# Loading K and V of a decode step in 32 transfers of 4 MB instead of 64 of 2 MB, with the second MLP matrix in four pieces instead of five

## The chip, the cores and the metric

The kernel runs on one core of a Trainium2 chip. The metric is the time of one execution on the device in microseconds (us); several executions are taken and the median is given. A core has a matrix engine (TensorE, here PE), a vector engine (DVE), a scalar engine (ACT), a general engine (POOL) and a queue engine (SP) that issues most of the transfers. Sixteen DMA engines carry every transfer between the chip's memory (HBM) and the core's on-chip memory (SBUF, 128 partitions); matmul results go to PSUM. A transfer is cut into packets that the sixteen engines work off, each in its own order, and its completion is counted engine by engine: the data may be used when the last of the sixteen is through.

## The reference

One decode step for eight sequences mixes sliding-window attention over a cache (branch A) with a small MLP (branch B), by a gate:

```
W = 2048; keys and values are the last W positions of caches of 8192
q = (x @ wq)                        # x: 8 x 576, wq: 576 x 4096 = 32 query heads of 128
scores = q . k / sqrt(128)          # 16 key/value heads, each serves 2 query heads
a = softmax(scores) @ v, then @ wo  # wo: 4096 x 576
b = gelu(layernorm(x) @ w1 + b1) @ w2 + b2     # w1: 576 x 4608, w2: 4608 x 576
out = g * a + (1 - g) * b,  g = sigmoid(sum(x * gate_w))
```

All inputs and the output are bf16. For each of 16 heads K is 8 batches x 2048 positions x 128 values, 4 MB (1 MB = 1,048,576 bytes here), and V the same: 128 MB together. wq is 4.5 MB, w1 and w2 5.06 MB each, wo 4.5 MB.

## The kernel before, in words

**Memory.** One large SBUF buffer, RAW, is cut into nine slots of SE = 8192 bf16 elements per partition (16 KB per partition, 2 MB over 128 partitions; L194, L195, L264, `slot` L338). At the start its lower part holds wq (slots 0 to 2) and w1 (from slot 3 on, L341 to L344); when the matmuls that read these are done (`o_qp` for wq, `o_hp` for w1), the slots take cache data. Slots 6 to 8 are free from the beginning.

**The stream.** A list (L557 to L565) fixes the order of all transfers on SP: six K units, then two V units, two K units and so on; after every eight V units comes a chunk of wo (W, 1.125 MB), and at the end the bias b2 and w2 (M) in pieces of 12, 12, 6, 4 and 2 rows per partition (`M_CUTS`, L564). A unit is one head and four of its eight batches: partition p holds the 64 consecutive positions x = p // 4 of batch p % 4, one contiguous run of 16,384 bytes (`src_of`, L580). Item n of the stream uses slot (n + 6) % 9 (`take_slot`, L584), so nine items share the nine slots in turn. SP issues the transfers in list order. Before each it waits until the former user of the slot is done (`slot_free`): for K that is the second of the unit's two transposes, for V the PV matmuls of the head, for wo and w2 their matmuls.

**K** (`k_unit`, L622): when a unit has landed, DVE transposes it in two steps (L641, 128 x 2048 fp32 words each) into one of two buffers KT, and PE multiplies each half with the queries (L650, L658 and, through a helper that keeps the loaded weights, L175). Four small POOL copies per unit (L634) lay out the queries for it; their source q4 is written by four ACT copies (L507). Scores of two heads (a group g: four units) share four PSUM banks.

**Softmax** (`softmax`, L589): after the fourth unit of a group, DVE takes the maximum (L592) and combines it (L595 to L601), ACT takes the exponential (L606), DVE transposes the result (L611), PE sums (L615). The next group's first score matmul waits for the exponentials, since the banks are shared.

**V** (`v_unit`, L670): after the second unit of a head PE multiplies the probabilities with both units (L684, 32 matmuls, `pv`). After the second head of a group, DVE and PE gather and scale the output (L697 to L707), and matmuls with wo (L550, `AccGroup`) add it to the result in PSUM. Matmuls with w2 (also L550) add to the same bank, a piece at a time as it lands. In the end the result is copied (L759, L760) and written out (L762).

**Order of work.** A planner (`_Plan.schedule`, L62) has an estimate of each operation's cost and of the transfers (428 GB/s) and lists every engine's operations by estimated earliest start, with a bonus for priority. The lists are fixed at build time; at run time each engine works through its own list in order and waits on semaphores where needed.

The selection matrices selv and seln (L459 to L464) and q4 carry the order in which batches lie on the partitions.

Of the kernel before, what the change touches and what calls it, by code (L numbers as in the profile page):

```python
# [181 lines left out]
def build_kernel(nc, A_x, A_k_cache, A_v_cache, A_wq, A_wo, B_x, B_w1, B_b1, B_w2, B_b2, gate_w, out):  # L182
# [8 lines left out]
    SCALE = float(Dh) ** -0.5  # L191
    HG = 2
    NG = Hkv // HG
    NSLOT = 9  # L194
    SE = 4 * W  # L195
    FC, FT = 4, 36
    FCW = 32 * FT
    HN = 3
# [10 lines left out]
    with ExitStack() as es:  # L209
# [51 lines left out]
        req("PT", 2 * 2048, BF)  # L261
        req("P", 2048, BF)
        req("KT", 2 * SE // 2, BF)
        req("RAW", NSLOT * SE, BF, 512)  # L264
        over("x_sb", "PT", 0, D, BF)
        over("gw_sb", "PT", 1152, D, BF)
        over("y_bf", "PT", 2304, D, BF)
# [67 lines left out]
        b1c = view("b1c", FC)  # L335

        def slot(s):
            return RAW[:, s * SE:(s + 1) * SE]  # L338

        wq_m = RAW[:, 0:4 * 4096].rearrange("p (t c) -> p t c", t=4)  # L340
        wq_r = RAW[:, 4 * 4096:4 * 4096 + 2048]  # L341
        W1O = 3 * SE
        w1_m = RAW[:, W1O:W1O + 4 * F].rearrange("p (t c) -> p t c", t=4)
        w1_r = RAW[:, W1O + 4 * F:W1O + 4 * F + F // 2]  # L344

# [11 lines left out]
        OC = 64  # L357

        eng_sems = {e: es.enter_context(nc.semaphore("sem_" + e)) for e in ENGS}
        dma_keys = ["x", "b", "b2", "wq", "w1", "out", "outb"] + ["s%d" % i for i in range(NSLOT)] + ["t%d" % i for i in range(4)]  # L360
        dma_sems = {k: es.enter_context(nc.semaphore("dma_" + k)) for k in dma_keys}

        P = _Plan()
# [92 lines left out]
        o_selv, o_seln = [], []  # L456
        for l in range(2):
            for h in range(2):
                for nm, lst in (("iqm", o_selv), ("i32", o_seln)):  # L459
                    def fn(e, l=l, h=h, nm=nm):  # L460
                        dst = bass.AP(arena_f, offset=foffs("selv" if nm == "iqm" else "seln") + 64 * l + 32 * h, ap=[[AST // 2, 128], [8, 4], [1, 8]])
                        src = bass.AP(arena_f, offset=foffs(nm) + 16 * l + h, ap=[[AST // 2, 128], [0, 4], [2, 8]])
                        return e.tensor_copy(dst, src)
                    lst.append(add("pool", fn, deps=[o_iqm] + o_i32, name="%s%d%d" % ("selv" if nm == "iqm" else "seln", l, h), cost=0.2, prio=-1))  # L464


        def held_x(e, out_of, lhs, rhs_of, n, t, first, last):
# [34 lines left out]

        o_q4 = []
        for he in range(4):
            def fn(e, he=he):
                src = bass.AP(ps, offset=BK_SEL * 512 + 8 * he, ap=[[PST, 128], [64, 16], [1, 8], [32, 2]])
                return e.activation(out=q4[:, he, :].rearrange("p (l b h) -> p l b h", l=16, b=8), in_=src, func=ACTF.Copy)  # L507
            o_q4.append(add("act", fn, deps=[o_selp], name="q4_%d" % he, cost=0.4))


        def h_fn(e):
# [42 lines left out]
                acc_groups.append(self)  # L554


        NUQ = 4 * NG  # L557
        stream = [("K", i) for i in range(6)]
        for vi in range(0, NUQ, 2):
            stream += [("V", vi), ("V", vi + 1)]  # L560
            if (vi + 2) % (NUQ // (Hq // WO_CH)) == 0:
                stream.append(("W", vi // (NUQ // (Hq // WO_CH))))
            stream += [("K", i) for i in (vi + 6, vi + 7) if i < NUQ]
        M_CUTS = [[12], [12], [6, 4, 2]]  # L564
        stream += [("B", 0)] + [("M", i) for i in range(len(M_CUTS))]  # L565

        last_dma = [d_w1r]
        slot_free = [[o_qp]] * 3 + [[o_hp]] * 3 + [[]] * 3
        n_slot = [0]
        tr_hist, qk_half = [], []  # L570
        qk_unit = {}
        exp_done, pt_done, pv_last = {}, {}, {}
        rg_done = {}
        o_item_ev = {}
        v_load, acc_ev, u_sum = {}, {}, {}
        b6_w, b6_r = [], [o_u]
        proj_ops = {}
        oT_done = {}

        def src_of(cache, g, q):  # L580
            hkv, b0 = 2 * g + q // 2, 4 * (q % 2)
            return cache[b0:b0 + 4, hkv, S0:Sk, :].rearrange("a (x r) d -> x a (r d)", x=32)

        def take_slot():  # L584
            n = n_slot[0]
            n_slot[0] += 1
            return (n + 6) % NSLOT

        def softmax(g):  # L589
            k = lambda i, n=1, parts=128, p0=0: sm[p0:p0 + parts, g, i:i + n]  # L590
# [28 lines left out]
            rg_done[g] = add("dve", lambda e: e.tensor_tensor(out=rg[:, g % 2:g % 2 + 1], in0=rr, in1=gcol, op=ALU.mult),  # L619
                             deps=[rc, o_gcol] + ([o_item_ev[g - 2]] if g >= 2 else []), name="rg_%d" % g, cost=0.16, prio=5)  # L620

        def k_unit(i):  # L622
            g, q = divmod(i, 4)
            s = take_slot()
            d = dma("sp", lambda e: e.dma_start(slot(s), src_of(A_k_cache, g, q)), "s%d" % s, 4 * W * Dh * 2, deps=slot_free[s], name="dk%d" % i, after=last_dma[-1:])
            last_dma.append(d)
            ub = q
            qrs = []
            for q_ in (q, q + 1) if q % 2 == 0 else ():
                for a in range(4):  # L630
                    def fn(e, a=a, q_=q_):
                        dst = bass.AP(arena, offset=32 * a * AST + aoffs("qbd") + q_ * 512 + 32 * a + 8 * q_, ap=[[AST, 32], [128, 4], [1, 8]])
                        src = bass.AP(arena, offset=32 * a * AST + aoffs("q4") + 32 * g + 8 * q_, ap=[[AST, 32], [256, 4], [1, 8]])
                        return e.tensor_copy(dst, src)  # L634
                    qrs.append(add("pool", fn, deps=o_q4 + [o_qz, qk_unit.get(4 * g + q_ - 4)], name="qr%d_%d" % (4 * g + q_, a), cost=0.2))
            trs = []
            for h in range(2):
                n = 2 * i + h
                kb = n % 2
                deps = [d] + ([qk_half[n - 2]] if n >= 2 else [o_selp])  # L640
                tr = add("dve", (lambda h=h, kb=kb: lambda e: e.transpose(bass.AP(arena_f, offset=foffs("KT") + kb * 2048, ap=[[AST // 2, 128], [1, 2048]]),  # L641
                                                                         bass.AP(arena_f, offset=foffs("RAW") + s * (SE // 2) + 32 * h, ap=[[AST // 2, 128], [64, 64], [1, 32]])))(),
                         deps=deps, name="tr%d_%d" % (i, h), cost=2.3, after=tr_hist[-1:])
                tr_hist.append(tr)
                trs.append(tr)

                def qk_fn(e, h=h, kb=kb):
                    mm = None
                    if q == 0 and h == 0:
                        e.matmul(ps[:, 0, :], maskL, maskR, start=True, stop=False)  # L650
                        for rc in range(1, 4):
                            held_matmul(nc, e, ps[:, rc, :], maskL, maskR, start=True, stop=False)
                    for ee in range(2):
                        for rc in range(4):
                            rhs = bass.AP(arena, offset=aoffs("KT") + kb * 4096 + rc * 1024 + ee, ap=[[AST, 128], [2, 512]])
                            args = (ps[:, rc, :], qbd[:, ub, 2 * h + ee, :], rhs)
                            last = q == 3 and h == 1 and ee == 1
                            mm = e.matmul(*args, start=False, stop=last) if rc == 0 else held_matmul(nc, e, *args, stop=last)  # L658
                    return mm
                deps = [tr] + qrs  # L660
                if q == 0 and h == 0:
                    deps += exp_done[g - 1] if g else o_q4 + [o_qs, o_mL, o_mR]
                qk = add("pe", qk_fn, deps=deps, name="qk%d_%d" % (i, h), cost=1.95 + (0.9 if q == 0 and h == 0 else 0), after=qk_half[-1:])
                qk_half.append(qk)
            qk_unit[i] = qk
            slot_free[s] = trs
            if q == 3:
                softmax(g)

        def v_unit(i):  # L670
            g, q = divmod(i, 4)
            s = take_slot()
            d = dma("sp", lambda e: e.dma_start(slot(s), src_of(A_v_cache, g, q)), "s%d" % s, 4 * W * Dh * 2, deps=slot_free[s], name="dv%d" % i, after=last_dma[-1:])  # L673
            last_dma.append(d)
            v_load[i] = (s, d)
            if i % 2 == 0:
                return

            def pv_fn(e):
                mm = None  # L680
                for t in range(16):
                    for j in (i - 1, i):
                        c = 32 * (j % 4)
                        mm = e.matmul(ps[c:c + 32, BK_OS[g % 2], :], PT[:, g % 2, 16 * c + 32 * t:16 * c + 32 * t + 32], slot(v_load[j][0])[:, 512 * t:512 * t + 512],  # L684
                                      start=(t == 0), stop=(t == 15), skip_group_check=True, tile_position=(0, c))
                return mm
            deps = [v_load[i - 1][1], d] + pt_done[g] + ([acc_ev[g - 2]] if g >= 2 else [o_u])
            prev = add("pe", pv_fn, deps=deps, name="pv%d" % i, cost=3.6, after=pv_hist[-1:])
            pv_hist.append(prev)
            slot_free[s] = slot_free[v_load[i - 1][0]] = [prev]  # L690
            if q == 3:
                pv_last[g] = prev
                for r in range(4):
# [15 lines left out]
                                 deps=[o_item_ev[g]], name="oT%d" % g, cost=0.25, prio=9)  # L709

        def wo_chunk(i):
            s = take_slot()
            h0 = WO_CH * i
            NT = WO_CH // WOR
            dst = slot(s)[:, 0:WO_CH * D].rearrange("p (t j c) -> p t j c", t=NT, j=WOR)
# [17 lines left out]
        def m2_chunk(ci):  # L733
# [12 lines left out]
                j, at = j + jn, at + jn  # L746
            slot_free[s] = ops

        pv_hist = []
        for kind, i in stream:  # L750
            {"K": k_unit, "V": v_unit, "W": wo_chunk, "M": m2_chunk, "B": bias}[kind](i)

        acc_ops = [g_.op for g_ in acc_groups]
        fin = []
# [78 lines left out]
```

## Time and profile before

| | |
|---|---|
| median of 3 runs | 367.55 us (367.52 to 367.84) |
| profiled execution | 367.57 us, its span 365.5 us |
| mean granted clock of PE | 0.860 |
| busy: PE / DVE / POOL / ACT | 246.3 / 225.7 / 36.1 / 31.9 us |
| HBM read | 154.31 MB, 422 GB/s over the span |
| K loads | 32, 2048 KB each, median 35.0 us from issue to landing |
| V loads | 32, 2048 KB each, median 33.4 us from issue to landing |

Here the page counts a KB as 1024 bytes and a MB as a million. "Busy" is time in which an engine worked; since engines overlap, the shares don't add up. The page's two lines of 40 digits or numbers cut the span into equal slices of 9.14 us: the DMA digits are the busy share of the sixteen DMA engines in tenths, GB/s is what they moved. "Issue to landing" includes the time that a transfer stands behind others in the queue. The chain of work is followed back from the last instruction, at each step to what released it. "SPq" and "PEq" stand for an engine's sequencer, where transfers are issued and waits take place.

### The profile page before, as it was taken

To read this page: it belongs to the slowest core of one execution; us is meant where nothing else is said; L and a number is where in the kernel's file an instruction comes from. 1 tells how busy PE (TensorE), PEld (TensorE's weight loads), DVE (VectorE), ACT (ScalarE), POOL (GpSimd) and SP (SyncE) were. 2 spreads that over 40 slices of the span, in tenths; PEclk is the share of its full clock that TensorE was granted. 3 is DMA by queue.
4 is the path that set the end of the run, shared out by engine and by line. 5 is a ranking of instruction groups with operands and counts; after the bars stand their busy time and mean duration, and the time that the engine had idled before them with its cause. 6 is when DMAs were issued, how large, how long until landed. Compare 5 with 4: busy or idle time off the path is not lost.

```text
span 365.5 us, 2939 instructions
## 1 busy us (share of the span) xinstructions
PE 246.3 (67%) x1350; PEld 57.8 (16%) x882; DVE 225.7 (62%) x285; ACT 31.9 (9%) x82; POOL 36.1 (10%) x156
## 2 busy tenths in 40 slices
PE   0338653899299838775599649865699569764675
PEld 0101000112021210202111220202111211112232
DVE  0725999576977776476658566575577764575010
ACT  1012102000300030003000300003000300003000
POOL 7121210010000100010010000010010000000000
PEclk9976998699679977998699867997599959899689
DMA  8999999999999999999999999999999999999995
GB/s 347 431 411 428 430 434 429 432 430 429 432 430 430 425 429 430 434 430 429 432 430 433 429 429 430 432 432 430 429 430 430 430 430 430 434 430 429 416 437 234
DMA packets 11702, 154.51 MB, mean 423 GB/s; under 512 B 1276, under 2 KB 1316, under 8 KB 2984
## 3 DMA queue, kind: packets, MB, share of 16 engines
q1 hardware_dynamic: 11632, 154.29, 99.0%
q8 instruction: 9, 0.15, 0.1%
q10 hardware_dynamic: 56, 0.03, 0.0%
q14 instruction: 5, 0.04, 0.0%
HBM read 154.31 MB, written 0.01 MB: 422 GB/s over the span
## 4 chain that ended last, share of the span: by engine, by line
DMA 73%; PE 14%; DVE 10%; issue 1%; SPq 1%; ACT 0%; DVEq 0%
DMA arena<-in_A_v_cache_dram 58%; DMA arena<-in_B_w_dram 15%; PE ps L684 9%; DVE arena L641 7%; PE ps L175 3%; PE ps L658 1%; DVE arena L592 1%; DVE arena L533 1%; PE ps L472 0%; SPq L673 0%; DVE arena L528 0%; DVE arena L532 0%; DVE arena L530 0%; PE ps L550 0%; ACT arena L526 0%
## 5 line engine op out<-in xcount | busy, mean ns | idle before, releaser
L641 DVE STREAM_TRANSPOSE arena<-arena 128x2048 f32<-128x2048 f32 x64 | 144.1, 2288 | 52.4 <-DMA arena<-in_A_k_cache_dram 28.7
L175 PE MATMUL ps<-arena 128*128 128x512 bf16 (+2 forms) x468 | 135.1, 441 | 0.0
L684 PE MATMUL ps<-arena 128*32 128x512 bf16 x512 | 67.1, 422 | 21.4 <-DMA arena<-in_A_v_cache_dram 21.4
L658 PE MATMUL ps<-arena 128*128 128x512 bf16 x128 | 54.2, 424 | 24.3 <-DVE arena L641 24.3
L634 POOL COPY arena<-arena 32x32 bf16<-32x32 bf16 x128 | 27.1, 211 | 240.5 <-PE ps L175 227.6
L606 ACT ACTIVATE arena<-ps,arena 128x512 bf16<-128x512 f32 x32 | 21.5, 685 | 233.0 <-DVE arena L601 233.0
L684 PEld LDWEIGHTS ps<-arena 128*32 128x32 bf16 x512 | 28.7, 105 | 68.1 <-issue 48.7
L658 PEld LDWEIGHTS ps<-arena 128*128 128x128 bf16 x128 | 13.5, 105 | 140.5 <-DVE arena L641 71.3
L592 DVE TENSOR_REDUCE arena<-ps 128x1 f32<-128x2048 f32 x8 | 18.3, 2287 | 12.8 <-PE ps L175 12.8
L611 DVE STREAM_TRANSPOSE arena<-arena 128x512 bf16<-128x512 bf16 x32 | 20.9, 689 | 5.1 <-ACT arena L606 5.1
L650 PE MATMUL ps<-arena 128*128 128x512 bf16 x8 | 4.6, 575 | 24.3 <-DVE arena L611 14.0
L697 DVE TENSOR_SCALAR arena<-ps,arena 128x128 f32<-128x128 f32 x8 | 2.7, 340 | 26.8 <-PE ps L684 26.8
L615 PE MATMUL ps<-arena 128*128 128x1 f32 x16 | 4.0, 317 | 18.4 <-DVE arena L614 18.4
L550 PE MATMUL ps<-arena 128*8 128x288 bf16 (+1 forms) x140 | 12.4, 316 | 4.7 <-DVE arena L707 2.9
L430 PE MATMUL ps<-arena 8*128 8x8 bf16 x8 | 0.6, 171 | 14.7 <-DVE arena L404 9.6
L698 DVE SCALAR_TENSOR_TENSOR arena<-ps,arena 128x128 f32<-128x128 f32 x24 | 8.4, 351 | 0.9
L615 PEld LDWEIGHTS ps<-arena 128*128 128x128 f32 x16 | 3.9, 287 | 24.7 <-DVE arena L614 21.4
L704 ACT ACTIVATE arena<-ps,arena 128x128 bf16<-128x128 f32 x8 | 2.9, 367 | 54.3 <-PE ps L700 54.3
L700 PE MATMUL ps<-arena 128*128 128x128 f32 x16 | 5.1, 414 | 3.4 <-DVE arena L617 1.8
L707 DVE STREAM_TRANSPOSE arena<-arena 128x128 bf16<-128x128 bf16 x8 | 2.5, 311 | 7.7 <-ACT arena L704 7.7
L550 PEld LDWEIGHTS ps<-arena 128*8 128x8 bf16 (+1 forms) x140 | 5.5, 90 | 9.1 <-DVE arena L707 4.1
L617 DVE RECIPROCAL arena<-ps 128x1 f32<-128x1 f32 x8 | 1.3, 168 | 8.9 <-PE ps L615 8.9
(82 smaller groups left out, 71.5 us busy)
## 6 DMA issues: line engine op xcount, KB each, us to landing
arena<-in_A_k_cache_dram SPq DMA_DIRECT2D x32, 2048.0 KB, 35.0
arena<-in_A_v_cache_dram SPq DMA_DIRECT2D x32, 2048.0 KB, 33.4
arena<-in_B_w_dram SPq DMA_DIRECT2D x1, 4608.0 KB, 23.4
arena<-in_A_wo_dram SPq DMA_DIRECT2D x4, 1152.0 KB, 36.3
arena<-in_A_wq_dram SPq DMA_DIRECT2D x1, 4096.0 KB, 13.0
arena<-in_B_w_dram SPq DMA_DIRECT2D x2, 1728.0 KB, 35.7
arena<-in_B_w_dram SPq DMA_DIRECT2D x2, 576.0 KB, 26.9
arena<-in_B_w_dram SPq DMA_DIRECT2D x1, 864.0 KB, 28.8
```

What stands on the lines that cost most here:

```text
L175: return e.add_instruction(mybir.InstMatmult(name=nc.get_next_instruction_name(), engine=mybir.EngineType.PE, ins=[e.lower_ap(rhs), e.lowe ...
L550: ins = e.matmul(ps[32 * j:32 * j + 8, BK_ACC, 0:JN], lhsT, rhs[:, JN * j:JN * j + JN], start=False, stop=True, skip_group_check=True, til ...
L592: mx = add("dve", lambda e: e.tensor_reduce(out=k(MX), in_=ps[:, 0:4, :].rearrange("p a n -> p (a n)"), axis=AXL.X, op=ALU.max), deps=[qk_ ...
L606: return e.activation(out=Pm[:, 512 * c:512 * c + 512], in_=ps[:, c, :], func=ACTF.Exp, bias=k(NB), scale=SCALE, accum_out=k(SUM + c))
L611: pts.append(add("dve", (lambda c=c: lambda e: e.transpose(bass.AP(arena, offset=aoffs("PT") + 2048 * (g % 2) + 128 * c, ap=[[AST, 128], [ ...
L615: sp_ = add("pe", lambda e: e.matmul(ps[:, BK_S, 0:1], seln, k(S), start=True, stop=True), deps=[s_] + o_seln + b6_r[-2:], after=b6_w[-1:] ...
L634: return e.tensor_copy(dst, src)
L641: tr = add("dve", (lambda h=h, kb=kb: lambda e: e.transpose(bass.AP(arena_f, offset=foffs("KT") + kb * 2048, ap=[[AST // 2, 128], [1, 2048]]),
L658: mm = e.matmul(*args, start=False, stop=last) if rc == 0 else held_matmul(nc, e, *args, stop=last)
L684: mm = e.matmul(ps[c:c + 32, BK_OS[g % 2], :], PT[:, g % 2, 16 * c + 32 * t:16 * c + 32 * t + 32], slot(v_load[j][0])[:, 512 * t:512 * t + ...
L698: return e.scalar_tensor_tensor(out=EV[:, g % 2, :], in0=src, scalar=maskr[:, r:r + 1], in1=EV[:, g % 2, :], op0=ALU.mult, op1=ALU.add)
L700: u_sum[g] = add("pe", lambda e: e.matmul(ps[:, BK_S, OC + 128 * (g % 2):OC + 128 * (g % 2) + 128], selv, EV[:, g % 2, :], start=True, sto ...
```

## The change

K and V of a head come as one transfer each, all eight batches. The slots become ND = 4 of DE = 2 x SE elements (32 KB per partition), and a fifth one of SE elements, number ND, which only the wo chunks use. Items of K, V and w2 take the four large slots in turn, in the order 1, 2, 0, 3. wq stays in the lowest 32 KB (now slot 0), w1 starts at slot 3 and reaches into the small slot, and the 64-row rest of wq follows it there. So slots 1 and 2 are free from the beginning, slot 0 after `o_qp`, slot 3 after `o_hp`.

A partition now holds two batches side by side: batch b of position block x lies on partition 4x + b // 2, in half b % 2. The order of batches in q4, selv and seln follows: q4 is written in eight ACT copies instead of four, selv and seln in 16 POOL copies instead of eight. A K item still makes two units (`k_item` calls `k_unit` twice), each reading its half of the slot, and the slot is free after all four transposes. The stream has the same order, two units at a time: K0, K1, K2, V0, K3, V1, K4, ..., with wo after V3, V7, V11 and V15. w2 comes as 24, 6, 4 and 2 rows.

```diff
-    NSLOT = 9
+    ND = 4
     SE = 4 * W
+    DE = 2 * SE
...
-        req("RAW", NSLOT * SE, BF, 512)
+        req("RAW", ND * DE + SE, BF, 512)
...
         def slot(s):
-            return RAW[:, s * SE:(s + 1) * SE]
+            return RAW[:, s * DE:min((s + 1) * DE, ND * DE + SE)]
...
-        W1O = 3 * SE
+        W1O = (ND - 1) * DE
+        WQR = W1O + 4 * F + F // 2
+        wq_r = RAW[:, WQR:WQR + 2048]
...
         for he in range(4):
-            def fn(e, he=he):
...
-                return e.activation(out=q4[:, he, :].rearrange("p (l b h) -> p l b h", l=16, b=8), in_=src, func=ACTF.Copy)
+            for u in range(2):
+                def fn(e, he=he, u=u):
...
+                    return e.activation(out=q4[:, he, :].rearrange("p (l u b h) -> p l u b h", l=16, u=2, b=4)[:, :, u, :, :], in_=src, func=ACTF.Copy)
...
-        stream = [("K", i) for i in range(6)]
-        for vi in range(0, NUQ, 2):
-            stream += [("V", vi), ("V", vi + 1)]
...
-        M_CUTS = [[12], [12], [6, 4, 2]]
+        NVW = Hkv // (Hq // WO_CH)
+        stream = [("K", 0), ("K", 1), ("K", 2)]
+        for vi in range(Hkv):
+            stream.append(("V", vi))
+            if (vi + 1) % NVW == 0:
+                stream.append(("W", vi // NVW))
+            if vi + 3 < Hkv:
+                stream.append(("K", vi + 3))
+        M_CUTS = [[24], [6, 4, 2]]
...
-        slot_free = [[o_qp]] * 3 + [[o_hp]] * 3 + [[]] * 3
+        slot_free = [[o_qp], [], [], [o_hp], [o_qp, o_hp]]
...
-            return (n + 6) % NSLOT
+            return (1, 2, 0, 3)[n % ND]
+
+        def load_item(cache, nm, hkv):
+            s = take_slot()
+            src = cache[:, hkv, S0:Sk, :].rearrange("b (x r) d -> x b (r d)", x=32)
+            d = dma("sp", lambda e: e.dma_start(slot(s).rearrange("p (u n) -> p u n", u=2), src), "s%d" % s, 8 * W * Dh * 2, deps=slot_free[s], name="%s%d" % (nm, hkv), after=last_dma[-1:])
+            last_dma.append(d)
+            slot_free[s] = []
+            return s, d
...
-            slot_free[s] = trs
+            slot_free[s] = slot_free[s] + trs
...
-            slot_free[s] = slot_free[v_load[i - 1][0]] = [prev]
+            slot_free[s] = [prev]
...
         def wo_chunk(i):
-            s = take_slot()
+            s = ND
...
+        def k_item(hkv):
+            s, d = load_item(A_k_cache, "dk", hkv)
+            for u in range(2):
+                k_unit(2 * hkv + u, s, d)
```

More of the change, by code (lines that the diff above doesn't have):

```diff
@@ L337, in slot @@
         def slot(s):
-            return RAW[:, s * SE:(s + 1) * SE]
+            return RAW[:, s * DE:min((s + 1) * DE, ND * DE + SE)]
         wq_m = RAW[:, 0:4 * 4096].rearrange("p (t c) -> p t c", t=4)
-        wq_r = RAW[:, 4 * 4096:4 * 4096 + 2048]
-        W1O = 3 * SE
+        W1O = (ND - 1) * DE
+        WQR = W1O + 4 * F + F // 2
+        wq_r = RAW[:, WQR:WQR + 2048]
         w1_m = RAW[:, W1O:W1O + 4 * F].rearrange("p (t c) -> p t c", t=4)
@@ L359, in build_kernel @@
         eng_sems = {e: es.enter_context(nc.semaphore("sem_" + e)) for e in ENGS}
-        dma_keys = ["x", "b", "b2", "wq", "w1", "out", "outb"] + ["s%d" % i for i in range(NSLOT)] + ["t%d" % i for i in range(4)]
+        dma_keys = ["x", "b", "b2", "wq", "w1", "out", "outb"] + ["s%d" % i for i in range(ND + 1)] + ["t%d" % i for i in range(4)]
         dma_sems = {k: es.enter_context(nc.semaphore("dma_" + k)) for k in dma_keys}
@@ L458, in build_kernel, with fn @@
             for h in range(2):
[L459 to L464, printed above, removed]
+                for u in range(2):
+                    for nm, lst in (("iqm", o_selv), ("i32", o_seln)):
+                        def fn(e, l=l, h=h, u=u, nm=nm):
+                            dst = bass.AP(arena_f, offset=foffs("selv" if nm == "iqm" else "seln") + 64 * l + 32 * h + u, ap=[[AST // 2, 128], [8, 4], [2, 4]])
+                            src = bass.AP(arena_f, offset=foffs(nm) + 16 * l + 8 * u + h, ap=[[AST // 2, 128], [0, 4], [2, 4]])
+                            return e.tensor_copy(dst, src)
+                        lst.append(add("pool", fn, deps=[o_iqm] + o_i32, name="%s%d%d%d" % ("selv" if nm == "iqm" else "seln", l, h, u), cost=0.2, prio=-1))
         def held_x(e, out_of, lhs, rhs_of, n, t, first, last):
@@ L504, in build_kernel @@
         for he in range(4):
-            def fn(e, he=he):
-                src = bass.AP(ps, offset=BK_SEL * 512 + 8 * he, ap=[[PST, 128], [64, 16], [1, 8], [32, 2]])
-                return e.activation(out=q4[:, he, :].rearrange("p (l b h) -> p l b h", l=16, b=8), in_=src, func=ACTF.Copy)
-            o_q4.append(add("act", fn, deps=[o_selp], name="q4_%d" % he, cost=0.4))
+            for u in range(2):
+                def fn(e, he=he, u=u):
+                    src = bass.AP(ps, offset=BK_SEL * 512 + 8 * he + u, ap=[[PST, 128], [64, 16], [2, 4], [32, 2]])
+                    return e.activation(out=q4[:, he, :].rearrange("p (l u b h) -> p l u b h", l=16, u=2, b=4)[:, :, u, :, :], in_=src, func=ACTF.Copy)
+                o_q4.append(add("act", fn, deps=[o_selp], name="q4_%d_%d" % (he, u), cost=0.3))
         def h_fn(e):
@@ L554, in __init__ @@
                 acc_groups.append(self)
-        NUQ = 4 * NG
-        stream = [("K", i) for i in range(6)]
-        for vi in range(0, NUQ, 2):
-            stream += [("V", vi), ("V", vi + 1)]
-            if (vi + 2) % (NUQ // (Hq // WO_CH)) == 0:
-                stream.append(("W", vi // (NUQ // (Hq // WO_CH))))
-            stream += [("K", i) for i in (vi + 6, vi + 7) if i < NUQ]
-        M_CUTS = [[12], [12], [6, 4, 2]]
+        NVW = Hkv // (Hq // WO_CH)
[7 more added lines that the diff above has]
+        M_CUTS = [[24], [6, 4, 2]]
         stream += [("B", 0)] + [("M", i) for i in range(len(M_CUTS))]
         last_dma = [d_w1r]
-        slot_free = [[o_qp]] * 3 + [[o_hp]] * 3 + [[]] * 3
+        slot_free = [[o_qp], [], [], [o_hp], [o_qp, o_hp]]
         n_slot = [0]
@@ L574, in build_kernel @@
         o_item_ev = {}
-        v_load, acc_ev, u_sum = {}, {}, {}
+        acc_ev, u_sum = {}, {}
         b6_w, b6_r = [], [o_u]
@@ L578, in build_kernel @@
         oT_done = {}
-        def src_of(cache, g, q):
-            hkv, b0 = 2 * g + q // 2, 4 * (q % 2)
-            return cache[b0:b0 + 4, hkv, S0:Sk, :].rearrange("a (x r) d -> x a (r d)", x=32)
         def take_slot():
@@ L620, in softmax, with k_unit @@
                              deps=[rc, o_gcol] + ([o_item_ev[g - 2]] if g >= 2 else []), name="rg_%d" % g, cost=0.16, prio=5)
-        def k_unit(i):
+        def k_unit(i, s, d):
             g, q = divmod(i, 4)
-            s = take_slot()
-            d = dma("sp", lambda e: e.dma_start(slot(s), src_of(A_k_cache, g, q)), "s%d" % s, 4 * W * Dh * 2, deps=slot_free[s], name="dk%d" % i, after=last_dma[-1:])
-            last_dma.append(d)
             ub = q
@@ L641, in k_unit @@
                 tr = add("dve", (lambda h=h, kb=kb: lambda e: e.transpose(bass.AP(arena_f, offset=foffs("KT") + kb * 2048, ap=[[AST // 2, 128], [1, 2048]]),
-                                                                         bass.AP(arena_f, offset=foffs("RAW") + s * (SE // 2) + 32 * h, ap=[[AST // 2, 128], [64, 64], [1, 32]])))(),
+                                                                         bass.AP(arena_f, offset=foffs("RAW") + s * SE + (q % 2) * (SE // 2) + 32 * h, ap=[[AST // 2, 128], [64, 64], [1, 32]])))(),
                          deps=deps, name="tr%d_%d" % (i, h), cost=2.3, after=tr_hist[-1:])
@@ L665, in k_unit, with v_item @@
             qk_unit[i] = qk
-            slot_free[s] = trs
+            slot_free[s] = slot_free[s] + trs
             if q == 3:
                 softmax(g)
-        def v_unit(i):
+        def v_item(hkv):
+            s, d = load_item(A_v_cache, "dv", hkv)
+            i = 2 * hkv + 1
             g, q = divmod(i, 4)
[L672 to L677, printed above, removed]
             def pv_fn(e):
@@ L683, in pv_fn @@
                         c = 32 * (j % 4)
-                        mm = e.matmul(ps[c:c + 32, BK_OS[g % 2], :], PT[:, g % 2, 16 * c + 32 * t:16 * c + 32 * t + 32], slot(v_load[j][0])[:, 512 * t:512 * t + 512],
+                        mm = e.matmul(ps[c:c + 32, BK_OS[g % 2], :], PT[:, g % 2, 16 * c + 32 * t:16 * c + 32 * t + 32], slot(s)[:, (j % 2) * SE + 512 * t:(j % 2) * SE + 512 * t + 512],
                                       start=(t == 0), stop=(t == 15), skip_group_check=True, tile_position=(0, c))
                 return mm
-            deps = [v_load[i - 1][1], d] + pt_done[g] + ([acc_ev[g - 2]] if g >= 2 else [o_u])
+            deps = [d] + pt_done[g] + ([acc_ev[g - 2]] if g >= 2 else [o_u])
             prev = add("pe", pv_fn, deps=deps, name="pv%d" % i, cost=3.6, after=pv_hist[-1:])
             pv_hist.append(prev)
-            slot_free[s] = slot_free[v_load[i - 1][0]] = [prev]
+            slot_free[s] = [prev]
             if q == 3:
@@ L711, in wo_chunk @@
         def wo_chunk(i):
-            s = take_slot()
+            s = ND
             h0 = WO_CH * i
@@ L747, in m2_chunk @@
             slot_free[s] = ops
+        def k_item(hkv):
+            s, d = load_item(A_k_cache, "dk", hkv)
+            for u in range(2):
+                k_unit(2 * hkv + u, s, d)
         pv_hist = []
         for kind, i in stream:
-            {"K": k_unit, "V": v_unit, "W": wo_chunk, "M": m2_chunk, "B": bias}[kind](i)
+            {"K": k_item, "V": v_item, "W": wo_chunk, "M": m2_chunk, "B": bias}[kind](i)
         acc_ops = [g_.op for g_ in acc_groups]
```

## The prediction

> **What bounds the kernel now.** I read the page first (slices, DMA queues), then the end of the chain of work, then the waits of SP's queue, then two stretches of the timeline: the start and the tail.
>
> ```profile
> span 365.5 us, 2939 instructions
> DMA  8999999999999999999999999999999999999995
> GB/s 347 431 411 428 430 434 429 432 430 429 432 430 430 425 429 430 434 430 429 432 430 433 429 429 430 432 432 430 429 430 430 430 430 430 434 430 429 416 437 234
> q1 hardware_dynamic: 11632, 154.29, 99.0%
> ```
>
> The sixteen DMA engines are busy from the second slice to the last at some 430 GB/s, and SP's queue alone fills 99.0% of their time. PE (67%) and DVE (62%) have room. The kernel ends when its bytes are in, plus a short tail, as the end of the chain shows (start, duration, what):
>
> ```profile
> 328.03 0.14 issue
> 328.17 3.64 PE ps L684 x32
> ...
> 333.05 29.68 DMA arena<-in_B_w_dram
> 362.73 0.04 issue
> 362.77 0.43 PE ps L550 x4
> ```
>
> The last piece of w2 lands at 362.73 and only 0.43 us of matmul follows before the output. Does the stream ever wait for a free slot? SP does, long and often, as its waits show (sum, times, longest):
>
> ```profile
> SPq L625 <- DVE arena L641: 96.1, 19, 11.7
> SPq L673 <- PE ps L684: 72.4, 12, 10.4
> ```
>
> but with transfers already queued: the V loads take 25.4 us at the least from issue to landing, against 4.87 us of transfer, so the queue never holds less than about 20 us of work. SP's waits cost nothing.
>
> **Part 1: 64 transfers of 2 MB become 32 of 4 MB.** V pairs land at 328.03, 337.77 and 347.49 (from the trace's record of DMA completions): 9.73 us per 4 MB, 4.865 per transfer. What of this belongs to the transfer rather than to its bytes? In the records of single packets a 16,384-byte packet takes 611 ns and a 36,864-byte one (w1) 1364; the slope, 753 ns for 20,480 bytes, is 27.2 bytes per ns, so the bytes of a packet are 602.4 ns. Packets of one engine start 607.2 ns apart, that is 4.8 ns per packet; the 4-byte packet that ends a transfer occupies the engine for 5.5 ns. Both sizes of transfer read 16,384-byte runs (one batch, 64 keys of 128 values), so the number of data packets stays. The W chunks show that a destination contiguous over two source runs is still moved run by run (1280 packets of 4,608 bytes). What goes is one 4-byte packet per engine for each of 33 transfers (32 of K/V, one of w2): 33 x 5.5 ns = 0.18 us. The 24-row w2 piece is one packet per partition where there were two: 8 packets per engine x 4.8 ns = 0.04 us. Together -0.22 us on the stream that sets the end. Bounds: nothing, if these packets overlap their neighbours, and, if all overhead belonged to the transfer, (4.865 - 8 x 0.6024) x 33 = -1.5 us. I take -0.2, because the packet records show it directly.
>
> The Trainium skill ("DMA: Bandwidth & Descriptors", Anatomy of one DMA) gives each transfer about 2.0 us of fixed cost (fitted for DMAs issued from GpSimd). Paid in series, 33 fewer would be 66 us; landings 4.865 us apart do not agree, and I give that no chance.
>
> **Part 2: slots.** A slot now frees 4 MB at once, and item n needs the slot of item n-4 (W has its own). Behind an item that has just landed lie three others, 3 x 9.73 = 29.2 us of stream. In steady state before, the second unit of a K head had its transposes (L641, 2.29 us each) done 4.5 to 14.7 us after it landed, and PV (L684) ended 3.8 to 8.8 us after the second V unit. The head's four transposes can no longer start with the first half, 4.87 us earlier: I add up to 2 x 2.3 = 4.6 us, so 9 to 20 us against 29.2. At least 9 us remain: cost 0. SP's longer issue (256 runs; the W issue with 256 runs takes 595 ns, a 2 MB one 535) is hidden under the same queue. Whatever stands behind a waiting load on SP (the next loads, W, b2) is late with it, which matters only when the queue runs dry.
>
> The start has the least room. On the timeline of DVE:
>
> ```profile
> 31.37 2.31 DVE L641 STREAM_TRANSPOSE arena<-arena 128x2048 f32<-128x2048 f32 x1 [8.75 <-DMA arena<-in_A_k_cache_dram]
> 33.79 1.36 DVE L528 TENSOR_TENSOR arena<-arena 128x1152 f32<-128x1152 f32 x1
> ...
> 49.29 8.91 DVE L641 STREAM_TRANSPOSE arena<-arena 128x2048 f32<-128x2048 f32 x4
> ...
> 70.81 4.50 DVE L641 STREAM_TRANSPOSE arena<-arena 128x2048 f32<-128x2048 f32 x2
> ```
>
> DVE was full from 31.4 to 58 with transposes and the gelu chain. After, K0 is whole only at 37.42 (the second unit's landing before). From there: 8 transposes of the first two heads 8 x 2.27 = 18.2, the last two gelu steps (L532 1.32, L533 2.29): 59.1, if nothing gaps, against 55.9. The steps up to the third head's last transpose (softmax, then PE at half clock) follow as before, 75.3 - 55.9 = 19.4 us: 78.5. That frees K2's slot for K4. K4 must be queued when V1 has passed, which landed at 85.95 on the slowest engine and 84.3 on the fastest; from issue to first packet about 1 us. So 4.8 to 6.5 us are left, or 1 to 3 if PE starts cold on K0 (idle from 32.6 to 39.7) and adds the 3.6 us of the two gelu steps as a gap. Cost taken 0; beyond about 85, from where the slowest engine would idle, every us is a us of span.
>
> **Part 3: the tail.** w2 now comes as 24 rows, then 6, 4, 2. On the timeline of PE:
>
> ```profile
> 355.58 2.13 PE L550 MATMUL ps<-arena 128*8 128x288 bf16 x32 [0.47 <-DVE arena L707]
> 358.59 1.64 PE L550 MATMUL ps<-arena 128*8 128x288 bf16 x24 [0.88 <-DMA arena<-in_B_w_dram]
> 360.68 0.90 PE L550 MATMUL ps<-arena 128*8 128x288 bf16 x12 [0.45 <-DMA arena<-in_B_w_dram]
> 362.07 1.11 PE L550 MATMUL ps<-arena 128*8 128x288 bf16 x12 [0.49 <-DMA arena<-in_B_w_dram]
> ```
>
> From 32 in 2.13 and 12 in 0.90: 61.5 ns per matmul and 0.16 us of latency. The 24 matmuls that ran inside the first burst (8 of wo, 24 of w2) now wait for 358.55, where the second twelve rows landed. From there 72 matmuls in a row: 358.59 + 0.16 + 72 x 0.0615 = 363.18, against 363.20 before (362.77 + 0.43). PE is then just level with the stream: the cover is used up. At the group's own mean, 2.13 / 32 = 66.6 ns, it is 363.54, +0.3. I take 0 to +0.3, +0.1 in the middle.
>
> **Part 4: the rest.** Eight more small POOL copies (L463, 0.21 us each, 1.26 us for eight overlapped) and q4 in eight ACT pieces instead of four (L507, 1.21 us for four; at most twice, to about 26.0). POOL's qr copies (L634) then end at about 26 + 4.1 = 30, before PE ends the first MLP matrix at 32.6 and before K0 at 37.4. Cost 0.
>
> Sum: -0.2 + 0.1 = -0.1 us. The profiled execution took 367.57 (span 365.5 and 2.07 around it), as good as the median 367.55. Forecast 367.4, with its own range 366.9 to 368.2. A difference under 0.2% (0.73 us) can hardly be told from no change here.
>
> **Rivals.**
> 1. Slower: the clock in the tail. PE now has nothing to do between 356.1 and 358.6, after a sparse stretch from 352.5. The granted clock drops after such gaps, as the busy times by stretch show (PE, PEld, DVE, ACT, POOL, then clock, DMA, GB/s):
>
> ```profile
> 344.50:347.50 3.00, 0.00 (x0) 0.00 (x0) 0.00 (x0) 0.00 (x0) 0.00 (x0) 0.94 0.93 393
> 347.50:352.50 5.00, 4.88 (x40) 2.21 (x40) 0.00 (x0) 0.00 (x0) 0.00 (x0) 0.69 1.05 443
> 355.50:358.50 3.00, 2.13 (x32) 1.35 (x32) 0.02 (x1) 0.00 (x0) 0.00 (x0) 1.00 0.95 405
> ```
>
> The clock records come in steps of 3.413 us; in this trace a step with PE under about 39% busy is followed by one at 0.5, and a full one by 1.0 again. If a whole step falls into the sparse stretch, about 28 of the 72 matmuls run at half speed, 28 x 61.5 ns = +1.7 us: 369.1. Against it: only some phases put such a step there, about 15 in 100, and a median over runs hides a few. Chance 0.12. The Trainium skill ("TensorE: Matmul & The Clock Gate", Part 1) says that the window is 3413 ns and free-running. The trace agrees on the length, but no run shown here varies the phase.
>
> 2. Slower: the queue runs dry before K4, when the third head's last transpose ends after 85 instead of 78.5 to 82. An order of DVE's work that puts the softmax later would do it: +0.8 to +4 us, say 369.4. Against it: 2 to 6 us of room. Chance 0.09.
>
> 3. Instruction fetches. Fourteen fetches of 8 or 16 KB run during the span on the same engines and delay the one they hit by 0.3 to 0.6 us. At the end the slowest engine is 1.91 us behind the fastest and 0.8 behind the mean. Spread otherwise, they give -0.8 to +0.6 us: 366.7 to 368.1. Chance 0.07 faster, 0.03 slower by over 0.2%.
>
> 4. Faster: the overhead does belong to the transfer, -1.5 us: 366.0. For it: 46 ns per transfer beyond the bytes. Against it: the packet records place 38 of them at the packets. Chance 0.08. That the change doesn't do what it says (other packets than 16,384 bytes) is within this and rival 3.
>
> **How the numbers follow.** Forecast 0.61; slower 0.12 + 0.09 + 0.03 = 0.24; faster 0.07 + 0.08 = 0.15. The range goes from 366.7 (rival 3's gain) to 369.4 (rival 1, and rival 2 up to +2), leaving out rival 4's end and the worse half of rival 2.
>
> **What would show it.** Right: K/V landings 9.71 to 9.73 us apart without a break, q1 near 99%, an end of the chain at w2 or at a run of L550 matmuls that ends within 0.3 us of the old time after the last landing. Wrong: a chain that goes through a K load issued after 85 us with fewer GB/s in slices 9 and 10 (rival 2); L550 at twice its 61.5 ns with a clock of 0.5 after 356 (rival 1); landings closer than 9.70 us (rival 4).

## The result

| | median (range) | executions | profiled: time, span |
|---|---|---|---|
| before | 367.56 us (367.51 to 367.84) | 6 | 367.57, 365.5 |
| changed | 369.48 us (368.74 to 370.13) | 6 | 369.98, 368.2 |

The ratio is 1.0046, with a 95% interval of 1.0034 to 1.0058: the changed kernel is slower by about 1.7 us by the ratio, 1.9 by the medians. Forecast was no change, 367.4 us; the time lies 0.08 us above the range's upper end of 369.4.

The profile of the changed kernel, the same lines of the page:

```profile
span 368.2 us, 2888 instructions
DMA  8999999999999999999999999999999999999992
GB/s 344 428 420 430 431 429 430 429 432 434 432 429 431 432 427 429 432 431 429 435 429 432 426 429 431 434 432 429 429 431 422 441 427 429 432 434 436 433 410 101
q1 hardware_dynamic: 10976, 154.29, 98.1%
```

The stream is as full as before up to the last slice. That one moves 101 GB/s instead of 234: the kernel goes on for longer after its bytes are in. The end of the chain (start, duration, what) says the same:

```profile
328.51 29.97 DMA arena<-in_B_w_dram
358.49 0.04 issue
358.53 7.45 PE ps L554 x66
365.98 0.02 issue
366.00 0.45 DVE arena L766
```

The 24 rows of w2 land at 358.49, where the second twelve rows landed before (358.54). From there PE, at L554 (L550 before), is the end of the kernel for 7.45 us. Its timeline in the tail:

```profile
353.17 0.41 PE L554 MATMUL ps<-arena 8*8 8x288 bf16 x4
354.04 1.07 PE L554 MATMUL ps<-arena 128*8 128x288 bf16 x8 [0.47 <-DVE arena L709]
358.53 7.43 PE L554 MATMUL ps<-arena 128*8 128x288 bf16 x72 [3.42 <-DMA arena<-in_B_w_dram]
```

The 72 matmuls take 7.43 us, 103 ns each, where the prediction had 61.5. Its busy times in steps of the granted clock (stretch, length, then PE, PEld, DVE, ACT, POOL busy, clock, DMA share, GB/s) name the reason:

```profile
350.74:354.15 3.41, 1.34 (x18) 0.48 (x10) 1.71 (x5) 0.37 (x1) 0.00 (x0) 1.00 1.00 430
354.15:357.56 3.41, 0.96 (x8) 0.27 (x4) 0.00 (x0) 0.00 (x0) 0.00 (x0) 0.50 0.92 393
357.56:360.98 3.42, 2.45 (x22) 1.38 (x24) 0.00 (x0) 0.00 (x0) 0.00 (x0) 0.50 0.92 379
360.98:364.39 3.41, 3.41 (x32) 1.89 (x30) 0.00 (x0) 0.00 (x0) 0.00 (x0) 0.50 0.16 59
```

PE was busy 1.34 of 3.41 us in the first step (39%); the next three have the clock at 0.50. The row of w2 matmuls, which starts at 358.53, runs at half clock until 364.39 and at the full one only after that. With 123 ns per matmul up to 364.39 and 61.5 from there on, it works out to end at 366.0; it ended at 365.95, against 363.18 before. The last landing is at 362.69 us, against 362.73 before, so all of the loss lies behind the last landing. In the kernel before, the steps ahead of the landing at 358.54 and around it were 77% and 61% busy, and the clock held:

```profile
353.97:357.38 3.41, 2.63 (x36) 1.73 (x38) 0.57 (x2) 0.37 (x1) 0.00 (x0) 1.00 1.00 426
357.38:360.80 3.42, 2.08 (x32) 1.09 (x30) 0.00 (x0) 0.00 (x0) 0.00 (x0) 1.00 0.96 400
```

SP's waits, which the prediction held to cost nothing, grew and still cost nothing:

```profile
SPq L593 <- DVE arena L647: 228.5, 15, 20.5
SPq L593 <- PE ps L686: 34.6, 11, 5.1
```

### The profile page after: what moved, and what is told of

The parts are those of the page before. It is cut to its first block, busy times and chain, and to the rows that moved or that the text cites. A ratio compares the mean times of both kernels' runs of the same rounds, so it can differ in the third digit from the quotient of the medians.

```text
span 368.2 us, 2888 instructions
## 1 busy us (share of the span) xinstructions
PE 244.3 (66%) x1350; PEld 55.5 (15%) x882; DVE 226.5 (61%) x285; ACT 32.1 (9%) x86; POOL 36.0 (10%) x164
## 4 chain that ended last, share of the span: by engine, by line
DMA 59%; DVE 24%; PE 15%; SPq 1%; issue 1%; ACT 0%; DVEq 0%
DMA arena<-in_A_k_cache_dram 51%; DVE arena L647 20%; DMA arena<-in_B_w_dram 8%; PE ps L175 7%; PE ps L686 3%; PE ps L664 2%; PE ps L554 2%; DVE arena L620 1%; DVE arena L537 1%; DVE arena L601 1%; DVE arena L536 0%; PE ps L656 0%; DVE arena L610 0%; DVE arena L700 0%; SPq L400 0%
## 5 line engine op out<-in xcount | busy, mean ns | idle before, releaser
L175 PE MATMUL ps<-arena 128*128 128x512 bf16 (+2 forms) x468 | 138.1, 448 | 0.0
L664 PE MATMUL ps<-arena 128*128 128x512 bf16 x128 | 55.6, 434 | 25.1 <-DVE arena L647 25.1
L686 PE MATMUL ps<-arena 128*32 128x512 bf16 x512 | 59.3, 385 | 1.3 <-DMA arena<-in_A_v_cache_dram 1.3
L640 POOL COPY arena<-arena 32x32 bf16<-32x32 bf16 x128 | 26.0, 203 | 244.3 <-PE ps L175 232.1
L686 PEld LDWEIGHTS ps<-arena 128*32 128x32 bf16 x512 | 24.6, 98 | 43.8 <-issue 16.4
L656 PE MATMUL ps<-arena 128*128 128x512 bf16 x8 | 4.8, 602 | 30.6 <-DVE arena L647 16.7
L554 PE MATMUL ps<-arena 128*8 128x288 bf16 (+1 forms) x140 | 14.9, 374 | 6.3 <-DMA arena<-in_B_w_dram 3.4
L554 PEld LDWEIGHTS ps<-arena 128*8 128x8 bf16 (+1 forms) x140 | 6.8, 105 | 12.0 <-DVE arena L709 4.1
L532 DVE TENSOR_TENSOR arena<-arena 128x1152 f32<-128x1152 f32 x1 | 1.4, 1357 | 11.1 <-ACT arena L530 11.1
```

The source lines that it names most:

```text
L175: return e.add_instruction(mybir.InstMatmult(name=nc.get_next_instruction_name(), engine=mybir.EngineType.PE, ins=[e.lower_ap(rhs), e.lowe ...
L554: ins = e.matmul(ps[32 * j:32 * j + 8, BK_ACC, 0:JN], lhsT, rhs[:, JN * j:JN * j + JN], start=False, stop=True, skip_group_check=True, til ...
```

## The experiments

Theory after the result: the clock falls in the gap that opens when twelve rows fewer are there to work on, and the 72 matmuls then run at half speed. Rivals: a long row of matmuls that each load weights is slow at any clock; or the 4 MB loads make something late, and the w2 cut is innocent. Runs 1 to 4 set theory and rivals against each other, on one chip, with 29 executions of the kernel before beside them: median 367.66, from 367.12 to 369.14.

**1. The w2 cut undone, the 4 MB loads kept.**

```diff
-        M_CUTS = [[24], [6, 4, 2]]
+        M_CUTS = [[12, 12], [6, 4, 2]]
```

Each piece of w2 has a semaphore of its own here.

> The changed kernel, but the 24 rows of w2 come as two transfers of 12 rows again, into the same large slot; K and V stay at 4 MB. Theory (the granted clock of PE falls in the gap before the 24 rows land, so the 72 matmuls behind them run at half speed): with 12 rows landing near 354.4 PE has work in the gap and is level with the stream again; the last w2 group ends by 363.3 in the span, 367.3 us (366.9 to 367.8). Rival (the 4 MB loads themselves make something late, and the w2 cut is innocent): the time stays near 369.5.

Measured: 367.53 us (367.22 to 367.62 in 12 executions), ratio 0.999 with the interval 0.9981 to 0.9999. The loss is gone, so the 4 MB loads and their slots are not its cause. The clock was not quite held in the profiled execution: from 358.73 on it was 0.5 for a step, but with only 48 matmuls left (they took 4.76 us) the end came at 363.48, 0.3 us later than before.

**2. The w2 cut alone, in the kernel before.** The 24 rows lie over two adjoining 2 MB slots, and both must be free:

```diff
-        M_CUTS = [[12], [12], [6, 4, 2]]
+        M_CUTS = [[24], [6, 4, 2]]
...
+            if ci == 0:
+                s_hi = take_slot()
+                assert s_hi == s + 1
+                room = RAW[:, s * SE:(s + 2) * SE]
+                free = slot_free[s] + slot_free[s_hi]
```

> The kernel before, with the one change that its first 24 rows of w2 come as one transfer over two adjoining 2 MB slots. Theory (clock): the gap lies between about 356 and 358.5, shorter than in the changed kernel, where PV had ended 1.6 us earlier; the clock falls in some executions and not in others, so 367.5 to 369.9 with a wide scatter; where L550 of the tail runs at over 100 ns per matmul, the clock is 0.5, where it runs at 61 to 67 ns, it is 1.0. Rival (72 matmuls in a row take 7.4 us whatever the clock): 369.9 in all runs. Rival (the 4 MB loads are needed for the loss): 367.5 in all runs.

Measured: 369.28 us (369.04 to 370.14 in 6 executions), ratio 1.0043 with the interval 1.0029 to 1.0057. The cut alone makes the whole loss, with 2 MB loads. I had expected it in some executions only; by their times it came in all six. Its clock steps (the row of 72 matmuls starts at 358.63):

```profile
353.69:357.11 3.42, 1.48 (x14) 0.66 (x14) 0.72 (x3) 0.37 (x1) 0.00 (x0) 1.00 0.95 408
357.11:360.52 3.41, 1.89 (x18) 1.00 (x20) 0.00 (x0) 0.00 (x0) 0.00 (x0) 0.50 0.92 381
360.52:363.93 3.41, 3.41 (x32) 1.84 (x30) 0.00 (x0) 0.00 (x0) 0.00 (x0) 0.50 0.32 122
```

A step with PE busy 43% (1.48 of 3.42 us) was followed by 0.50. The prediction had put the border at 39%. With half clock until 363.93 the row works out to end at 365.79, and that is where it ended.

**3. The 24 rows kept, PE kept busy.** 6 matmuls on zeros after the last PV, 13 between the last wo group and the w2 rows, into a PSUM bank that nobody reads any more:

```diff
+        def warm(n):
+            def fn(e):
+                mm = None
+                for _ in range(n):
+                    mm = e.matmul(ps[:, 0, :], zeros_bf, ones_bf, start=True, stop=True)
+                return mm
+            return fn
```

> The changed kernel with 24 rows in one transfer, and 19 added matmuls on zeros into a free PSUM bank, 6 after the last PV and 13 after the last wo group, so that PE has little idle time before the 24 rows land. Theory (clock): the 72 matmuls run at 61 to 67 ns each and end at 363.2 to 363.6, 367.4 to 367.9 us; granted clock 1.0 from 355 on. Rival (a long row of matmuls with a weight load each is slow by itself): still 7.4 us, 369.5 us or more.

Measured: 367.32 us (367.17 to 367.59 in 11 executions), a little under the expected range; ratio 0.9983 with the interval 0.9972 to 0.9995. The timeline of PE in its tail:

```profile
355.13 2.98 PE L680 MATMUL ps<-arena 128*128 128x512 bf16 x13
358.68 4.61 PE L554 MATMUL ps<-arena 128*8 128x288 bf16 x72 [0.58 <-DMA arena<-in_B_w_dram]
```

and its clock from the landing on:

```profile
358.50:363.00 4.50, 4.32 (x70) 3.07 (x72) 0.00 (x0) 0.00 (x0) 0.00 (x0) 1.00 0.62 253
```

The same 72 matmuls behind the same transfer take 4.61 us instead of 7.43. Added work took 2.2 us off the median of the changed kernel. The rival, a row that is slow by itself, falls: the row's rate went with the clock, and in the changed kernel and run 2 the clock steps account for its whole length.

**4. The transfers by themselves.** Run 1 with each K or V item as two transfers of 2 MB into the same 4 MB slot, both awaited before use:

```diff
-            d = dma("sp", lambda e: e.dma_start(slot(s).rearrange("p (u n) -> p u n", u=2), src), ...
+            for u in range(2):
...
+                d = dma("sp", (lambda srcu=srcu, u=u: lambda e: e.dma_start(slot(s)[:, u * SE:(u + 1) * SE], srcu))(), ...
```

> The kernel of the first run of this set (w2 as 12 + 12), with each K or V item as two transfers of 2 MB into the same 4 MB slot, both awaited before use: 32 transfers more, nothing else. Theory (a transfer costs an engine 5.5 ns): the sixteen engines end 0.18 us later in the mean than in the first run, time the same within 0.4 us, 367.4. Rival (46 ns per transfer): 1.5 us later, 368.8.

Measured: 367.4 us (367.01 to 369.22 in 12 executions), ratio 0.9996 with the interval 0.9984 to 1.0008: no difference in the time. Two of the twelve took 368.63 and 369.22; they were not profiled, and what held them up is open. The size is read from the trace instead: the mean over the sixteen DMA engines of when the last transfer was through, less the same for the rest of w1. It is 335.50 us in run 1 and 335.69 with the halves: 0.19 us for 32 transfers, 6 ns each. These are one profiled execution each, and kernels with like transfers differ by up to 0.08 us in this measure. The rival's 1.5 us falls.

**5 and 6. The clock held up in both kernels.** A second set, on another chip (23 executions of the kernel before: 367.64, from 367.09 to 369.16). Run 5 is run 1 with 14 matmuls on zeros (6 after the last PV, 8 between the first and second twelve rows), run 6 the kernel before with 9 (6 and 3); the edit is that of run 3.

> K and V at 4 MB, w2 as 12, 12, 6, 4, 2 rows, and 14 added matmuls on zeros into a free PSUM bank: 6 after the last PV, 8 between the first and the second twelve rows of w2. Theory (stream 0.2 us shorter in the mean of the engines, clock held up in the tail): the last matmul ends 0.4 to 0.5 us after the last landing in every execution, 367.2 us (367.0 to 367.5), the least of the kernels so far by a little. Rival (the added matmuls delay the second twelve rows): 367.6 or more.

> The kernel before with 9 added matmuls on zeros, 6 after the last PV and 3 between the first and the second twelve rows of w2. Theory: the kernel before loses now and then to the clock in its tail too (its executions beside the first set reach from 367.1 to 369.1); held up, its median stays within 0.3 us of 367.6, its upper end comes down below 368. What is left between this kernel and the one above is what the 4 MB transfers are worth by themselves: 0.1 to 0.3 us by the packet records. Rival (the upper executions come from instruction fetches or from the stream): the upper end stays at 369.

Measured: run 5 367.40 us (366.95 to 367.56 in 12 executions), ratio 0.9988 (0.9978 to 0.9998); run 6 367.45 us (367.04 to 367.91 in 12), ratio 0.9991 (0.9981 to 1.0001). Run 5 lies in its expected range but is not the least so far (run 3: 367.32, on the first chip). The upper executions of the kernel before, up to 369.16, are gone from run 6 as expected. That fits the clock but doesn't show it: none of those upper executions was profiled, and with 4 of 23 executions above 368 us, twelve in a row below it come about once in ten by chance. In run 5's tail, as in that of the kernel before, each piece of w2 is done before the next one lands:

```profile
358.59 1.64 PE L554 MATMUL ps<-arena 128*8 128x288 bf16 x24
360.70 0.90 PE L554 MATMUL ps<-arena 128*8 128x288 bf16 x12 [0.47 <-DMA arena<-in_B_w_dram]
362.07 1.12 PE L554 MATMUL ps<-arena 128*8 128x288 bf16 x12 [0.47 <-DMA arena<-in_B_w_dram]
```

Between runs 5 and 6 lie 0.05 us: what the 4 MB transfers are worth by themselves cannot be told in the time. Runs 1, 3 and 5 are 0.1 to 0.2% faster than the kernel before, with intervals that end just under 1. That this comes mainly from the clock is likely but not shown, since run 6, which has the clock alone, ends at 1.0001.

**7. One slot fewer.** Run 1 with three large slots:

```diff
-    ND = 4
+    ND = 3
...
-        slot_free = [[o_qp], [], [], [o_hp], [o_qp, o_hp]]
+        slot_free = [[o_qp], [], [o_hp], [o_qp, o_hp]]
...
-            return (1, 2, 0, 3)[n % ND]
+            return (1, 0, 2)[n % ND]
```

> K and V at 4 MB, w2 as 12, 12, 6, 4, 2 rows, but three large slots instead of four, so that two items instead of three lie behind one that has just landed. Theory (a late slot costs nothing until the queue is dry, then us for us): in steady state the slots came free 4 to 17 us after landing, against 19.4 us of queue, so no loss there; at the start the third K item's slot came free 20.3 us after landing (76.9), and V1 now needs it, with the queue dry at 76: 1 to 3 us lost once, 368.4 to 370.5, one longer gap between landings near 76 to 80 us and none later. Rival (the slots are the reason for the loss of the changed kernel): several gaps, 375 us or more.

Measured: 375.27 us (374.57 to 377.14 in 4 executions), ratio 1.0218 (1.0186 to 1.0249). SP's timeline at the start, and the busy times around it:

```profile
58.58 0.60 SPq L593 DMA_DIRECT2D arena<-in_A_k_cache_dram  x1
77.94 0.60 SPq L593 DMA_DIRECT2D arena<-in_A_v_cache_dram  x1
78.59 0.61 SPq L593 DMA_DIRECT2D arena<-in_A_k_cache_dram  x1
```

```profile
66.00:76.00 10.00, 8.40 (x32) 1.70 (x19) 6.22 (x10) 1.46 (x6) 0.78 (x4) 0.64 0.83 356
76.00:80.00 4.00, 3.83 (x30) 1.19 (x22) 1.92 (x1) 0.00 (x0) 0.04 (x1) 1.00 0.24 66
80.00:90.00 10.00, 8.67 (x38) 0.86 (x9) 8.89 (x4) 0.00 (x0) 1.62 (x8) 1.00 0.98 418
```

The place was right: V1, issued at 77.94, when the transfer before it had landed at 76.18. The price was not. V1 landed 14.15 us after its predecessor and K4 11.01 after V1, where 9.69 is the normal distance: 5.8 us lost for an issue 1.8 us late. Those 1.8 us count from the slowest engine. In the mean the sixteen engines were through with the transfer before V1 at 74.92, their first packets of V1 start at 79.35 and later, 1.4 us after the issue, and most of these take about 1.0 us instead of 0.61. So an engine stood idle for some 4.5 us. Of the rest, 1.3 us is one engine that finished K4 at 101.34, 1.3 us after the next slowest; why is open. The distances of later landings are 9.67 to 9.9, or 12.5 to 13.1 with a wo chunk between, as in the changed kernel, but for two of 10.47 (one is V11, issued 2.6 us ahead of the end of the queue); together some 1.6 us, and I did not follow them. My 1 to 3 us was too small. The rival had the size right, 375, but its "several gaps" is not what the trace shows.

## Why the prediction was wrong

**The stream: right.** It had -0.22 us from 33 fewer transfers and fewer packets. By the mean of the sixteen engines from the end of w1 to the end, the four kernels with 2 MB transfers (before, runs 2, 4 and 6) took 335.67 to 335.75 us, the four with 4 MB and four slots (changed, runs 1, 3 and 5) 335.44 to 335.50: -0.24. In the last landing little of it is seen (362.69 against 362.73), since the slowest engine is 2.22 us behind the fastest instead of 1.91. That would fit rival 3's instruction fetches, but no run tests it. Run 4 measures 0.006 us for a further transfer in a full queue. The Trainium skill ("DMA: Bandwidth & Descriptors", Anatomy of one DMA) has about 2.0 us of fixed cost per transfer, fitted for DMAs issued from GpSimd. The loads here are issued from SP, and run 4 shows no such cost between transfers that stand in the queue. Of the 1280 packets of 4,608 bytes that the prediction cites for the W chunks, 1024 are theirs; the reading stands.

**The slots: right.** In steady state K's slots were free again, and the next load issued, 9 to 17 us after the former K item had landed (predicted 9 to 20), V's after 4 to 8. At the start the first two heads' transposes ended at 58.5 (predicted 59.1; its terms add up to 59.2) and the third head's at 76.9 (predicted 78.5 to 82); V1 landed 8.8 us after K4 had been issued.

**The tail: the term was right at full clock and the clock was wrong.** The sum priced the 72 matmuls at 61.5 ns, full clock; they took 103. The mechanism stood in the prediction, as rival 1, but with a chance of 0.12. The step that failed is the sentence there that only some phases, about 15 in 100, put a step of the clock into the sparse stretch. By their times, all six executions of the changed kernel and all six of run 2 paid for it.

Two things went into that mistake. The border was read as 39% busy from the trace of before. There the busiest step that was followed by half clock had 39%, and the least busy one that kept the full clock had 48%; no step lay between, and run 2 has one at 43% that was followed by 0.50. And only whole steps inside the sparse stretch were counted, where a step that holds the idle time and the first matmuls of the row can be as sparse and slow the rest of the row. An estimate with the prediction's own tail (the PE rows of before, with the 24 matmuls moved behind the landing): with the border at 39%, some step below it slows part of the row in about 6 of 10 phases; at 44%, in every phase. The phase does vary: the profiled executions have the edge of a step at 350.56 (before), 350.74 (changed), 351.29 (run 4) and 351.90 (run 1).

The sparse stretch itself was copied from the kernel before, from 352.5. In the changed kernel it begins at 351.1: its last softmax was later, so PE worked on the last but one PV until 346.3 and ran the last one at full clock, 3.6 us instead of 5.1. PE then had 1.97 us of work in the 7.4 us up to the landing. That made it worse but is not needed for the loss: in run 2 the stretch begins at 352.6, much as predicted.

**The size of rival 1: too small.** One step at half speed was counted, 28 matmuls, +1.7 us. The clock came back only after a full step. The landing falls into a step, which is then 72% busy (357.56 to 360.98) and does not bring it back; the half clock lasted until 364.39, 5.9 us of work. That makes 7.43 - 4.61 (run 3) = 2.8 us in the profiled execution, and 1.2 to 2.6 us over the median of before in the six timed. The Trainium skill ("TensorE: Matmul & The Clock Gate", Part 1) has the clock fall after an idle window of about 3.4 us. Here a window with PE 39% or 43% busy was enough.

With the clock held, the prediction's arithmetic stands: 0.16 + 72 x 0.0615 = 4.59 us, and run 3 took 4.61; its time was 367.32 where 367.4 was forecast.

## What to carry to other kernels

Where a kernel ends on a stream, the last transfers also decide when the matrix engine has something to do: merging two of them saves nanoseconds, and the gap it opens can halve the clock for the work that then stands on the path. Cost the tail at half clock whenever the engine is less than about half busy in the 3.4 us steps before it. If the gap can't be closed with real work, a few matmuls on zeros may close it, as 19 of them did here (run 3). Count the distance from issue to the end of the queue, not SP's waiting time: the waits grew and cost nothing until the queue ran dry.

## What was not expected of the hardware

- The clock fell without an idle step. Over the nine traces, every 3.41 us step at full clock with PE under 39% busy was followed by half clock and none above 45% was; in between both occur (39% kept it in run 2, 42% in run 7, 43% lost it in run 2).
- PE got the full clock back only after a step with much work in it. No step under 67% busy did it. From 67 to 84% both occur (67% did in run 7, 72% did not in the changed kernel, 79% did not in run 6), and near 26 us steps of 93% (before) and 99% (changed) did not, against the prediction's reading that a full step brings it back. So the busy share alone does not settle it, and what else does is open. A row of matmuls that begins in the middle of a step stayed at half clock for the rest of it and the whole next one: 5.9 us.
- A dry queue cost more than its lateness: 5.8 us for 1.8 us (run 7). Most engines had run dry before the slowest one, and the first packets started 1.4 us after the issue. The late transfer took 12.4 us from issue to landing, where 9.7 is the normal distance of two landings.
- The 4-byte packet that ends a transfer was nearly all that a further transfer cost in a full queue: 6 ns per engine by run 4, 5.5 by the packet records.
